# Attention and gated MLP on one core: a written-out engine order planned with other costs, another order of tanh and exp, and another start

## The chip, the cores and the metric

The kernel runs on one core of a Trainium2 chip. The time is device microseconds (us) of one execution, taken as the median of several. Before the change it is 603.34 us, the median of 3 runs (602.14 to 603.51).

## What is computed

Attention with capped scores over 4 batches, 12 heads, 448 positions and 64 features, and on its result a gated MLP with 768 features in, 1536 hidden and 768 out:

```python
scores = (q @ k.T) / sqrt(64)              # per batch and head, 448 x 448
scores = cap * tanh(scores / cap)
attn = exp(scores - scores.max(-1, keepdims=True))
attn = attn / (attn.sum(-1, keepdims=True) + 1e-09)
x = (attn @ v).transpose(0, 2, 1, 3).reshape(4 * 448, 768)
g = x @ w_gate
out = (g * (1 / (1 + exp(-g))) * (x @ w_val)) @ w_out
```

## The kernel before

**The work.** The 24 pairs of heads are taken two at a time in 12 "quads". A quad has 7 score tiles of 128 keys by 2 x 448 queries: three for each of the two pairs (numbers 1 to 6) and one shared by both for the last 64 keys (number 0, `MID`), which comes last. Of each tile TensorE makes the scores (`qk`, L886, float32) in one of two PSUM buffers `sc`; ScalarE takes the tanh of them (`tanh`, L890), which frees the buffer, and then the exponential (`exp`, L893). TensorE multiplies the exponentials with the values (`av`, L831, and `avt`, L912, for the shared tile), and sums them over the keys with ones (`sum`, L918) after VectorE has added three tiles together (`sa`, L813 and L815). VectorE empties the products' PSUM buffers (`xk`, L257); the sums go by DMA through a reshaping (`rl`, tile `r`), a reciprocal on VectorE (`rec`, L932) and two more DMAs (`rs`, `rld`) back to a multiplication on VectorE (`x`, L849).

On TensorE the order in the attention is a chain: after the first score tile of a quad come the `av` of the previous quad's first pair, then two score tiles, the `av` of its second pair, a score tile, the sums, two score tiles, `avt`, and the shared score tile.

The MLP follows, in float16 with high and low parts (L528 to L530: three products for each), by a fast matrix scheme of 7 products in place of 8, in 12 rounds for the first two matrices, then two passes for the third (L703 to L705). Its weights are read as 64-bit floats, narrowed to 32 bits on ScalarE and VectorE (`nA`, `nB`, `nC`, `n1`), stored to DRAM (`st`) and loaded again (`ld`, L466), then split in high and low halves (`wH` on ScalarE or VectorE, `wL` on VectorE). The narrowing of the first weights lies beside the attention.

**The order.** Class `Plan` lays all operations out by a list scheduling before anything is emitted. Each has a duration per engine that may do it, a priority (a time at which it is wanted), the operations that it waits for, and buffers that it takes. At each step the planner looks at the earliest start that any ready operation could have, and among those within 0.05 us of it takes the one with the earliest priority. The result is the order of instructions of every engine (SyncE issues nearly all the DMAs), and the engines keep it: an instruction that waits holds back all behind it on its engine. Durations and lags of the plan are constants of the code: `LAG` and `LAT` from the end of one operation to the start of another, `SWITCH` when TensorE goes to another kind of work, `ISSUE` for what one DMA operation costs on SyncE, `FAR` for what it takes longer to land. The grid of priorities in the attention is `QUAD` us to a quad.

**The start.** `warm` sends 9 products of a constant tile to TensorE (L294), gives the first 128 columns of the first keys to ScalarE's DMA queue (L280), and the load of the others follows the first queries on SyncE's (L789, L796).

**Buffers of the exponentials.** Each tile of a quad has a place among 11 (`w0` to `w5` and five `B` tiles), handed out at L764 to L773; the last quad uses `B` tiles only.

Of the kernel before, what the change touches and what calls it, by code (L numbers as in the profile page):

```python
# [8 lines left out]
F32 = mybir.dt.float32  # L9
# [7 lines left out]
P = 128  # L17
C = 112
S = 448
B = 4  # L20
# [19 lines left out]
WARM = 9  # L40


QUAD = 13.5
TAIL = 9.0
AHEAD = 14.0
NEAR = 4
# [8 lines left out]
NARROW_B = 40.0  # L55
NARROW_STEP_B = 7.4
HLOAD = {(0, 0): -14.0, (1, 0): -9.0, (0, 1): -4.0, (1, 1): 0.0}
SWITCH = 0.17


NARROWED = [4, "u", 5, "u", 6, "u", 7, 8, "u", 9, 10, "u", 11, "u"]
# [18 lines left out]
class Plan:  # L80


    LAT = 0.2
    LAG = {
        ("PE", "PE"): 0.0, ("ACT", "ACT"): 0.13, ("DVE", "DVE"): 0.13, ("POOL", "POOL"): 0.13, ("ACT", "DVE"): 0.16,
        ("DVE", "POOL"): 0.16, ("ACT", "POOL"): 0.18, ("POOL", "ACT"): 0.07, ("POOL", "DVE"): 0.08, ("ACT", "PE"): 0.25,
    }

    FAR = {"rl": 1.4, "rs": 1.4, "rld": 1.4}
    ISSUE = {"rld": 0.96}  # L90
    BIAS = {}
    SHIFT = dict.fromkeys(("c1", "c11", "cu", "c5", "c22", "c12", "oc1", "oc11", "ocu", "oc5", "oc22", "oc12", "wL", "wH"), -20.0) | {"gt": -20.0, "ga": -20.0, "va": -20.0, "sa": -15.0, "cp": -15.0, "rec": -15.0, "xk": -30.0}

# [10 lines left out]
    def run(self):  # L104
# [69 lines left out]
        while ready:  # L174
            t0, cands = 1e18, []
            for k in ready:
                o = ops[k]
                r = room(o) if o["alloc"] else 0.0
                if r is None:
                    continue  # L180
                best = None
                for t, d, e, x in o["opts"]:
                    s = max(t, r, free[e])
                    if e == "PE" and kind(k) != last:
                        s += SWITCH
                    c = s + x
                    if best is None or c < best[0]:
                        best = c, s, d, e
                cands.append((best[1], o["prio"], best[2], best[3], k))
                t0 = min(t0, best[1])  # L190
            if not cands:
                raise RuntimeError("the buffers do not suffice")
            s, _, d, e, k = min((c for c in cands if c[0] <= t0 + 0.05), key=lambda c: (c[1], c[0]))
            o = ops[k]
            if e == "SP":
                b = max(s + 1.125, dma_free)
                free[e] = s + self.ISSUE.get(k[0], 0.48)
                dma_free = b + d
                end[k] = dma_free + 0.73 + self.FAR.get(k[0], 0.0)
            else:  # L200
                free[e] = s + d
                end[k] = s + d
                if e == "PE":
                    last = kind(k)
            eng[k] = e
            for tag, readers in o["alloc"]:
                held[tag].append(readers)
            order.append((s, len(order), k, e))
            o["start"] = s
            o["eng"] = e  # L210
            del ready[k]
            for u in users.get(k, ()):
                nleft[u] -= 1
                if nleft[u] == 0:
                    enter(u)
# [6 lines left out]
def tile_capped_attention_gated_mlp(ctx: ExitStack, tc: tile.TileContext, qd, kd, vd, cap, eye, w1, w2, out):  # L222
# [21 lines left out]
    def st(shape, dtype, tag):  # L244
        return pool(tag).tile(shape, dtype, tag=tag, name=tag, bufs=BUFS[tag])
# [29 lines left out]
    icapr = nc.scalar.alloc_register("icapr")  # L275

    def warm():
        u = QUADS[0][0]
        T["rk", u] = st([P, S], F32, "c10")
        nc.scalar.dma_start(T["rk", u][:, :P], kd[u][:, :P])  # L280
        nc.scalar.dma_start(cap1[:, 0:1], cap)
        nc.gpsimd.dma_start(capb, cap.to_broadcast([P, 1]))
        z = nc.const_aps.tensor(1.0, (P, S), mybir.dt.bfloat16)
        nc.gpsimd.memset(ones, 0.0)
        for i in range(2):
            nc.gpsimd.memset(ones[:, 48 * i : 48 * i + 16], 2.0**-X_UP)
            nc.gpsimd.memset(ones[D * i : D * i + D, D + 16 * i : D + 16 * i + 16], 2.0**-X_UP)
        nc.gpsimd.memset(sq, 0.0)
        y = const.tile([P, 1], F32, name="tiny")
        nc.vector.memset(y, 0.0)  # L290
        nc.scalar.activation(y, y, AF.Tanh)
        o = pt([P, 512], "av")
        for i in range(WARM):
            nc.tensor.matmul(o[:, :S], lhsT=z[:, :P], rhs=z, start=True, stop=True)  # L294
# [29 lines left out]
        op(key, prio, {"ACT": us}, fn, deps + [spare])  # L324


    mm_us = 6 * 188 / 1000.0
    pair_us = 10.6 * mm_us / 7
    quad_at = [6.0 + QUAD * q for q in range(len(QUADS))]
    t = quad_at[-1] + QUAD + TAIL  # L330
# [92 lines left out]
    def blocks(w):  # L423
        g0, g1 = 2 * w * NCC, (2 * w + 1) * NCC
        for c in range(HALF):
# [14 lines left out]
            for p, (_, _, _, z) in PROD.items():  # L440

                def high(e, z=z, c=c):
                    T["xs", z, w, c] = x_half(("XH", z, w, c), home(z, w, c))
                    copy(e, T["xs", z, w, c][:, 0], T["raw", z, w, c])

                def low(e, z=z, c=c):
                    sub(e, T["xs", z, w, c][:, 1], T["raw", z, w, c], T["xs", z, w, c][:, 0])

                raw = ("x", {"B11": g0 + c, "B21": g0 + c + HALF, "B22": g1 + c + HALF}[z]) if z[0] == "B" else (z, w, c)
                order = prod_at[w, w, p] - AHEAD + 0.3 * c  # L450
                op(("XH", z, w, c), order, {"ACT": 0.57, "DVE": 0.39}, high, [raw], [(home(z, w, c), [("p", LAST[w], w, p)])])
                op(("XL", z, w, c), order + 0.01, {"DVE": 0.62}, low, [("XH", z, w, c)])
                if z in PLAIN:
                    n = 3 * PLAIN.index(z) + c
                    square(("qx", z, w, c), 2, win_at[3] + 10.0 * n + 5.0 * w, 0.58, lambda z=z, c=c: T["xs", z, w, c][:, 0], [("p", 3 + n // 2, 1, 4)], ("XH", z, w, c))

    def step(s):
        f, ws = STEPS[s]
# [44 lines left out]
            op(key("S", n), at[1 if n < 3 else 2] - [0, 12.5, 11.3, 13.8, 12.6][n], {"DVE": 0.52}, lambda e, n=n: comb(e, n), deps, alloc)  # L503
        for half in range(2):
            if 1 in ws:
                square(key("q", half), 0, at[0] - 6.0 + 2.0 * half, 0.85, lambda half=half: gate(half).rearrange("p a b -> p (a b)"), full[half], ("XH", "B11", s // NFC, 0))
        last = [2, 5, 3, 4]
        for n in range(4):
            tw = at[n] - 8.8
# [6 lines left out]
        for w in ws:  # L516
# [40 lines left out]
            for b in range(2):  # L557
# [19 lines left out]
                op(key("gt", w, b), z + 1.0, {"ACT": 0.56}, gt, [k("c12" if b else "c11")], [("th", [key("va", w, b)])])  # L577
                deps = [key("gt", w, b), k("c22")] + ([] if b else [("p", s, w, 4)])
                op(key("va", w, b), max(end + 0.2, z + 2.2), {"DVE": 0.62}, va, deps)
                square(("qh", g, f), 3, max(end, z + 2.0) + 1.0, 0.58, lambda b=b, w=w: T["cc", s, w, b], [key("va", w, b)], ("XH", "B11", 0, 0) if s < NFC - 1 else ("oH", 0, 1, 0))  # L580
                op(("hst", g, f), max(end, z + 2.0) + 1.2, {"SP": 0.64}, hst, [key("va", w, b)])

    NP = NDM // 2
# [23 lines left out]
    def outs(pr):  # L607
# [54 lines left out]
        for n, (p, d) in enumerate(OUT_ORDER):  # L662
# [11 lines left out]
            dep = [("st", "o", a, d, j) for j in range(2)]  # L674
            op(("ld", "o", pr, p, d), tp - 24.0, {"SP": 1.09}, load, dep, [(home_, [("wL", "o", pr, p, d)] + [("qo", p, d)] * pr)])
            if pr:
                square(("qo", p, d), 1, tp - 6.5, 0.85, lambda p=p, d=d: T["wf", "o", 1, p, d].rearrange("p a b -> p (a b)"), [("ld", "o", 1, p, d)], ("oH", 1, p, 0))

            def wH(e, p=p, d=d, n=n):
                T["wh", "o", pr, p, d], T["wl", "o", pr, p, d] = w_slots(wtag(4 * len(STEPS) + n))  # L680
# [75 lines left out]
    def spot(q, i):  # L756

        return (i - 1) % NT
# [2 lines left out]

        return quad_at[q] + (QUAD * (1.3 + 0.3 * n) if q < len(QUADS) - 1 else QUAD + 2.0 + 2.3 * n)

    TAGS, idle = {}, [f"w{n}" for n in range(6)] + ["B60", "B61", "B62", "B70", "B71"]  # L764
    for q in range(len(QUADS)):
        if q == len(QUADS) - 1:
            idle = [x for x in idle if x[0] == "B"] + ["B22", "B32", "B52"]
        old = TAGS.get(q - 1, [])
        TAGS[q] = [None] * NT
        for i in sorted(range(NT), key=lambda i: spot(q, i)):  # L770
            TAGS[q][i] = idle.pop(0)
            if old and i in (2, 4, MID):
                idle += [x for x in {2: old[1:4], 4: old[4:], MID: old[:1]}[i] if x[0] == "B" or q < len(QUADS) - 1]  # L773

    def pair(u, q):
        upper = u == QUADS[q][1]
# [12 lines left out]
            nc.sync.dma_start(T["rq", u], qd.rearrange("n p s -> (n p) s")[z : z + P])  # L789

        def loadk(e):
            if not joint and (q or upper):
                T["rk", u] = st([P, 6, P], F32, "wf").rearrange("p a b -> p (a b)")[:, :S] if upper else st([P, S], F32, f"c1{q % 2}")

            z = slice(0 if q or upper else P, S)
            nc.sync.dma_start(T["rk", u][:, z], kd[u][:, z])  # L796

        qks = sorted([("qk", q, i) for i in [MID] + own], key=lambda x: spot(q, x[2]))
        slot = lambda n: [(f"A4{q % 3}" if joint else "wf" if upper else f"c{n}{q % 2}", qks)]
# [59 lines left out]
    def quad(q):  # L859
# [12 lines left out]
        op(("loadv", q), quad_at[q] - 4.0, {"SP": 1.6}, loadv, alloc=[(f"B4{q % 2}", [("avt", q)])])  # L872

        for i in range(NT):
            tag = TAGS[q][i]

            def qk(e, i=i):
                z = T["sc", q, i] = pt([P, 2, 512], "sc")
# [23 lines left out]
            op(("qk", q, i), z, {"PE": 0.75}, qk, deps, [("sc", [("tanh", q, i)])])  # L902
            users = [("av", w[0], (i - 1) % 3)] if i != MID else [("avt", q)]
            users += [("sum", q)] if i == MID else [("sa", w[0], (i - 1) % 3 // 2)]
            op(("tanh", q, i), z + 1.0, {"ACT": 0.92}, tanh, [("qk", q, i)], [(tag, users)])
            op(("exp", q, i), z + 2.8, {"ACT": 0.95}, expo, [("tanh", q, i)])

        def avt(e):
            for h in range(2):
# [27 lines left out]

        tz = av_at(q, 2) + 2.0
        op(("avt", q), av_at(q, 2) - 0.5, {"PE": 0.75}, avt, [("exp", q, MID), ("loadv", q), ("av", u, 2), ("av", v, 2)])
        op(("sum", q), av_at(q, 2), {"PE": 1.15}, sums, [("sa", u, 1), ("sa", v, 1), ("exp", q, MID)], [("b2", [("cp", q)])])  # L940
        op(("cp", q), av_at(q, 2) + 1.0, {"DVE": 0.35}, part, [("sum", q)], [(f"c2{q % 2}", [("rl", q)])])
        op(("rl", q), tz + 0.1, {"SP": 0.2}, rl, [("cp", q)], [("r7", [("rs", q)])])
        op(("rec", q), tz + 3.0, {"DVE": 0.2}, rec, [("rl", q)])
# [154 lines left out]
    for q in range(len(QUADS) + 1):  # L1098
        now = [("qk", q, i) for i in sorted(range(NT), key=lambda i: spot(q, i))] if q < len(QUADS) else []
        if not q:  # L1100
            line += now
            continue
        u, v = QUADS[q - 1]
        avs = lambda z: [("av", z, j) for j in range(3)]
        line += now[:1] + avs(u) + now[1:3] + avs(v) + now[3:4] + [("sum", q - 1)] + now[4:6] + [("avt", q - 1)] + now[6:]
    for a, b in zip(line, line[1:]):
        plan.ops[b]["deps"].append(a)
    order = plan.run()
# [140 lines left out]
```

## Time and profile before

| | |
|---|---|
| median of 3 runs | 603.34 us |
| the profiled execution | 604.18 us |
| its span, first to last instruction | 602.3 us |
| TensorE matmul busy | 591.7 us, 98% |
| VectorE busy | 505.9 us, 84% |
| ScalarE busy | 418.4 us, 69% |
| chain that ended last | PE 84%, DMA 6%, DVE 5%, ACT 2% |

PE is TensorE (PEld its weight loads), DVE is VectorE, ACT is ScalarE, POOL is GpSimd, SP is SyncE; SPq is SP's own queue of DMA issues. "L886" is line 886 of the kernel. A matmul counts as busy until its modelled end, and consecutive matmuls overlap, so the busy time of PE says less than the starts of its rows.

### The profile page before, as it was taken

Reading aid. Unit: us, or ns where it says so; the run is one execution under the profiler, and the core shown is the slowest. Engines: PE = TensorE matmul, PEld = TensorE weight load, DVE = VectorE, ACT = ScalarE, POOL = GpSimd, SP = SyncE. Lnnn points to the kernel's source line nnn. Section 1 sums busy time; section 2 is a strip of 40 time slices with the busy share of each in tenths; the row PEclk is TensorE's granted clock in tenths of the full one; section 3 lists DMA queues with packets and bytes.
Section 4 is the critical chain, followed back from the end, with each engine's and each line's share of the span. In section 5 each row is a group of like instructions: output and inputs, shape, how many; then the busy total and the mean of one; then the engine's idle time right before and its main releaser. Section 6 shows DMA issues by size and latency. Waiting matters only on the chain.

```text
span 602.3 us, 9584 instructions
## 1 busy us (share of the span) xinstructions
PE 591.7 (98%) x3333; PEld 279.8 (46%) x3333; DVE 505.9 (84%) x869; ACT 418.4 (69%) x725; POOL 1.6 (0%) x11
## 2 busy tenths in 40 slices
PE   7999999999999999999999999999999999999997
PEld 2333333333345555555555555555455555555553
DVE  2678899899898998888989888989979999898840
ACT  6999989899858855756648476656757766685611
POOL 1000000000000000000000000000000000000000
PEclk9999999999999999999999999999999999999999
DMA  8676676755423365877786766586968598546121
GB/s 252 207 237 192 186 223 212 217 153 149 126 86 101 125 173 153 265 203 229 198 239 215 217 211 190 171 274 206 347 235 319 170 331 287 192 135 234 35 78 66
DMA packets 69598, 118.08 MB, mean 196 GB/s; under 512 B 13604, under 2 KB 47524, under 8 KB 69541
## 3 DMA queue, kind: packets, MB, share of 16 engines
q1 hardware_dynamic: 69362, 117.32, 61.4%
q8 instruction: 28, 0.46, 0.3%
q14 instruction: 30, 0.24, 0.1%
q10 hardware_dynamic: 146, 0.07, 0.0%
q0 software_dynamic: 32, 0.00, 0.0%
HBM read 81.79 MB, written 35.48 MB: 195 GB/s over the span
## 4 chain that ended last, share of the span: by engine, by line
PE 84%; DMA 6%; DVE 5%; ACT 2%; SPq 2%; issue 1%; ACTq 0%; DVEq 0%
PE b L528 10%; PE b L530 10%; PE b L529 10%; PE sc L886 7%; PE b L704 7%; PE b L703 7%; PE b L705 7%; PE av L831 6%; PE om L528 4%; PE om L530 4%; PE om L529 4%; DMA w<-w 3%; DMA r<-c 2%; PE b L918 2%; PE av L912 1%; PE om L704 1%
## 5 line engine op out<-in xcount | busy, mean ns | idle before, releaser
L528 PE MATMUL b<-A,w 128*128 128x448 f16 x252 | 88.8, 352 | 0.4 <-ACT c L255 0.4
L529 PE MATMUL b<-A,w 128*128 128x448 f16 x252 | 88.8, 352 | 0.0
L530 PE MATMUL b<-A,w 128*128 128x448 f16 x252 | 88.8, 352 | 0.0
L528 PEld LDWEIGHTS <-w 128*128 128x128 f16 x504 | 49.3, 98 | 46.8 <-issue 0.7
L529 PEld LDWEIGHTS <-w 128*128 128x128 f16 x504 | 49.3, 98 | 46.4 <-issue 0.7
L530 PEld LDWEIGHTS <-w 128*128 128x128 f16 x504 | 49.3, 98 | 46.0
L255 ACT ACTIVATE c<-b 128x448 f32<-128x448 f32 x54 | 29.0, 538 | 44.4 <-PE b L705 22.9
L528 PE MATMUL om<-B,w 128*128 128x448 f16 x144 | 50.8, 352 | 0.0
L529 PE MATMUL om<-B,w 128*128 128x448 f16 x144 | 50.8, 352 | 0.0
L530 PE MATMUL om<-B,w 128*128 128x448 f16 x144 | 50.8, 352 | 0.0
L886 PE MATMUL sc<-c,c 64*128 64x448 f32 (+1 forms) x192 | 45.2, 577 | 2.4 <-ACT w L890 1.5
L546 DVE TENSOR_TENSOR c<-c,b 128x448 f32<-128x448 f32 x60 | 37.1, 619 | 8.6 <-PE b L530 3.2
L262 DVE TENSOR_TENSOR A<-A,A 128x448 f16<-128x448 f32 (+3 forms) x55 | 43.7, 823 | 0.1
L255 ACT ACTIVATE w<-B 128x768 f16<-128x768 f32 x32 | 26.9, 840 | 22.9 <-PE b L705 17.9
L890 ACT ACTIVATE w<-sc 128x896 f32<-128x896 f32 x42 | 36.9, 917 | 7.2 <-PE sc L886 7.0
L890 ACT ACTIVATE B<-sc 128x896 f32<-128x896 f32 x42 | 36.9, 921 | 5.0 <-PE sc L886 4.9
L262 DVE TENSOR_TENSOR w<-B,w 128x768 f16<-128x768 f32 x39 | 37.0, 953 | 2.2 <-ACT w L255 2.2
L893 ACT ACTIVATE B<-B 128x896 f32<-128x896 f32 x42 | 38.4, 959 | 0.1
L893 ACT ACTIVATE w<-w 128x896 f32<-128x896 f32 x42 | 38.2, 955 | 0.1
L704 PE MATMUL b<-A,w 128*128 128x448 f16 x108 | 38.1, 352 | 0.0
L528 PE MATMUL b<-B,w 128*128 128x448 f16 x108 | 38.1, 352 | 0.0
L530 PE MATMUL b<-B,w 128*128 128x448 f16 x108 | 38.1, 352 | 0.0
(138 smaller groups left out, 1233.3 us busy)
## 6 DMA issues: line engine op xcount, KB each, us to landing
w<-w SPq DMA_DIRECT2D x72, 384.0 KB, 3.7
hidden<-c SPq DMA_DIRECT2D x48, 224.0 KB, 3.1
B<-w_S SPq DMA_DIRECT2D x24, 384.0 KB, 4.3
w<-wf SPq DMA_DIRECT2D x16, 384.0 KB, 4.9
B<-w SPq DMA_DIRECT2D x15, 384.0 KB, 3.4
th<-parts SPq DMA_DIRECT2D x48, 112.0 KB, 2.9
A<-hidden SPq DMA_DIRECT2D x12, 448.0 KB, 5.7
B<-hidden SPq DMA_DIRECT2D x12, 448.0 KB, 3.8
```

What stands on the lines that cost most here:

```text
L255: nc.scalar.activation(out_, in_, AF.Copy, scale=1.0 if scale is None else scale)
L262: ENG[e].tensor_tensor(out_, a, b, op=ALU.subtract)
L528: nc.tensor.matmul(o, lhsT=wh, rhs=xh, start=first, stop=False, skip_group_check=True)
L529: nc.tensor.matmul(o, lhsT=wl, rhs=xh, start=False, stop=False, skip_group_check=True)
L530: nc.tensor.matmul(o, lhsT=wh, rhs=xl, start=False, stop=end, skip_group_check=True)
L546: nc.vector.tensor_tensor(z, z, T["ps", s, w, b][:, :S], op=ALU.add)
L703: nc.tensor.matmul(o, lhsT=wh, rhs=xh, start=first, stop=False, skip_group_check=True)
L704: nc.tensor.matmul(o, lhsT=wl, rhs=xh, start=False, stop=False, skip_group_check=True)
L705: nc.tensor.matmul(o, lhsT=wh, rhs=xl, start=False, stop=end, skip_group_check=True)
L886: nc.tensor.matmul(z[rows, h, :S], lhsT=T["rk", w][r, keys], rhs=T["rq", w][r], start=True, stop=True)
L890: nc.scalar.activation(T["t", q, i], T["sc", q, i][:, :, :S], AF.Tanh, scale=icapr)
L893: nc.scalar.activation(T["t", q, i], T["t", q, i], AF.Exp, scale=capr)
```

## The change

The planner's constants are replaced, the priority of `exp` moves from 2.8 to 5.0 us behind its tile's grid time, the places of the exponentials become a plain ring of 11, and the last quad uses seven `B` tiles. The keys of the first pair are loaded whole by SyncE behind the queries. The 9 warm passes read a tile of zeros that VectorE fills.

```diff
-QUAD = 13.5
+QUAD = 13.1
-SWITCH = 0.17
+SWITCH = {"sc": 0.206, "av": 0.15, "sh": 0.16, "sum": 0.0, "mm": 0.16}
     LAT = 0.2
-    LAG = {
-        ("PE", "PE"): 0.0, ("ACT", "ACT"): 0.13, ("DVE", "DVE"): 0.13, ("POOL", "POOL"): 0.13, ("ACT", "DVE"): 0.16,
-        ("DVE", "POOL"): 0.16, ("ACT", "POOL"): 0.18, ("POOL", "ACT"): 0.07, ("POOL", "DVE"): 0.08, ("ACT", "PE"): 0.25,
-    }
-    FAR = {"rl": 1.4, "rs": 1.4, "rld": 1.4}
-    ISSUE = {"rld": 0.96}
+    LAG = {("PE", "PE"): 0.0, ("ACT", "PE"): 0.08, ("DVE", "PE"): 0.08}
+    LAG |= {(a, b): 0.04 for a in ("ACT", "DVE") for b in ("ACT", "DVE")}
+    OVERLAP = {"ACT": 0.1, "DVE": 0.085}
+    FAR = {"rl": 2.0, "rs": 2.0, "rld": 2.0, "ld": 1.5}
+    ISSUE = {"rld": 1.26, "loadv": 2.45, "rl": 0.65, "rs": 0.4, "ld": 0.45, "st": 0.54}
...
-                        s += SWITCH
+                        s += SWITCH[last]
...
-                free[e] = s + self.ISSUE.get(k[0], 0.48)
+                free[e] = s + self.ISSUE.get(k[0], 0.48) * (2 if k[0] == "loadq" and d > 1.0 else 1)
...
-                free[e] = s + d
+                free[e] = s + d - self.OVERLAP.get(e, 0.0)
...
     def warm():
-        u = QUADS[0][0]
-        T["rk", u] = st([P, S], F32, "c10")
-        nc.scalar.dma_start(T["rk", u][:, :P], kd[u][:, :P])
...
-        z = nc.const_aps.tensor(1.0, (P, S), mybir.dt.bfloat16)
+        z = st([P, 2 * S], F32, "B20").bitcast(mybir.dt.bfloat16)[:, :S]
+        nc.vector.memset(z, 0.0)
...
-    mm_us = 6 * 188 / 1000.0
+    mm_us = 6 * 189 / 1000.0
...
-    TAGS, idle = {}, [f"w{n}" for n in range(6)] + ["B60", "B61", "B62", "B70", "B71"]
-    ...
+    RING = [*(f"w{n}" for n in range(6)), "B60", "B61", "B62", "B70", "B71"]
...
-            z = slice(0 if q or upper else P, S)
-            nc.sync.dma_start(T["rk", u][:, z], kd[u][:, z])
+            nc.sync.dma_start(T["rk", u], kd[u])
...
-            tag = TAGS[q][i]
+            tag = (["B22", "B32", "B52", "B60", "B61", "B62", "B70"][spot(q, i)] if q == len(QUADS) - 1 else RING[(NT * q + spot(q, i)) % len(RING)])
...
-            op(("tanh", q, i), z + 1.0, {"ACT": 0.92}, tanh, [("qk", q, i)], [(tag, users)])
-            op(("exp", q, i), z + 2.8, {"ACT": 0.95}, expo, [("tanh", q, i)])
+            op(("tanh", q, i), z + 1.0, {"ACT": 0.917}, tanh, [("qk", q, i)], [(tag, users)])
+            op(("exp", q, i), z + 5.0, {"ACT": 0.953}, expo, [("tanh", q, i)])
...
-        op(("sum", q), av_at(q, 2), {"PE": 1.15}, sums, ...
+        op(("sum", q), av_at(q, 2), {"PE": 1.27}, sums, ...
```

The planned durations of the squares that watch the range of the numbers grow by 0.08 us as well. TensorE's chain in the attention is the same.

## Rows read from the trace of the kernel before

**Rows 1.** Waits of PE in two stretches, 15 to 168 us and 168 us on.

```profile
PE sc L886 <- ACT B L890: 0.8, 1, 0.8
PE av L831 <- DVE B L257: 0.6, 1, 0.6
PE av L831 <- DVE A L257: 0.5, 1, 0.5
...
PE b L528 <- ACT c L255: 0.4, 1, 0.4
```

**Rows 2.** Windows: stretch, its length, busy (count) by engine, PEclk, DMA share, GB/s.

```profile
158.00:171.00 13.00, 11.65 (x89) 4.41 (x89) 13.00 (x22) 10.89 (x18) 0.00 (x0) 1.00 0.32 97
...
300.00:400.00 100.00, 100.00 (x530) 51.72 (x529) 88.71 (x175) 62.99 (x154) 0.00 (x0) 1.00 0.69 216
```

**Rows 3.** Timeline of PE: start, us, engine, line, operation, count.

```profile
0.78 3.52 PE L294 MATMUL av<-const-bfloat16-1.0 128*128 128x448 bf16 x9 [0.78 <-PEq L1238]
4.22 3.91 PE L886 MATMUL sc<-c,c 64*128 64x448 f32 x12
...
14.96 1.02 PE L886 MATMUL sc<-c,c 64*128 64x448 f32 x4
...
28.02 1.02 PE L886 MATMUL sc<-c,c 64*128 64x448 f32 x4
...
80.26 1.02 PE L886 MATMUL sc<-c,c 64*128 64x448 f32 x4
...
93.92 1.02 PE L886 MATMUL sc<-c,c 64*128 64x448 f32 x4
...
106.98 1.02 PE L886 MATMUL sc<-c,c 64*128 64x448 f32 x4
...
120.41 1.02 PE L886 MATMUL sc<-c,c 64*128 64x448 f32 x4
...
168.09 0.36 PE L528 MATMUL b<-A,w 128*128 128x448 f16 x1
```

**Rows 4.** Timeline of ACT over the first quad.

```profile
6.14 0.92 ACT L890 ACTIVATE w<-sc 128x896 f32<-128x896 f32 x1 [2.90 <-PE sc L886]
7.21 0.92 ACT L890 ACTIVATE w<-sc 128x896 f32<-128x896 f32 x1 [0.16 <-PE sc L886]
8.02 1.78 ACT L893 ACTIVATE w<-w 128x896 f32<-128x896 f32 x2
9.70 0.91 ACT L890 ACTIVATE w<-sc 128x896 f32<-128x896 f32 x1
...
13.07 1.73 ACT L890 ACTIVATE w<-sc 128x896 f32<-128x896 f32 x2
```

**Rows 5.** Groups by line: busy us, mean ns | idle before; the nearest to a fill.

```profile
L257 DVE CAST A<-A 128x448 f16<-128x448 f32 x15 | 5.4, 385 | 0.0
...
L288 POOL MEMSET sq<- 128x192 f32 x1 | 0.3, 258 | 0.1
...
L290 DVE MEMSET tiny<- 128x1 f32 x1 | 0.1, 59 | 0.8 <-PEq L1238 0.8
```

**Rows 6.** DMA issues: one SP row, and two of KB and median us to landing.

```profile
1.19 0.41 SPq L796 DMA_DIRECT2D c<-kd  x1
...
c<-kd SPq DMA_DIRECT2D x11, 224.0 KB, 4.2
...
c<-kd SPq DMA_DIRECT2D x1, 160.0 KB, 2.9
```

**Rows 7.** Waits of all engines, 145 to 170 us.

```profile
DVE w L257 <- DMA wf<-w: 2.0, 1, 2.0
ACT w L255 <- DMA wf<-w: 1.6, 1, 1.6
```

**Rows 8.** Chain of work that ended last, in order of time: start, us, what.

```profile
67.41 6.07 DMA r<-c
...
148.60 3.72 DMA wf<-w
```

More of the change, by code (lines that the diff above doesn't have):

```diff
@@ L454, in blocks @@
                     n = 3 * PLAIN.index(z) + c
-                    square(("qx", z, w, c), 2, win_at[3] + 10.0 * n + 5.0 * w, 0.58, lambda z=z, c=c: T["xs", z, w, c][:, 0], [("p", 3 + n // 2, 1, 4)], ("XH", z, w, c))
+                    square(("qx", z, w, c), 2, win_at[3] + 10.0 * n + 5.0 * w, 0.66, lambda z=z, c=c: T["xs", z, w, c][:, 0], [("p", 3 + n // 2, 1, 4)], ("XH", z, w, c))
     def step(s):
@@ L505, in step @@
             if 1 in ws:
-                square(key("q", half), 0, at[0] - 6.0 + 2.0 * half, 0.85, lambda half=half: gate(half).rearrange("p a b -> p (a b)"), full[half], ("XH", "B11", s // NFC, 0))
+                square(key("q", half), 0, at[0] - 6.0 + 2.0 * half, 0.93, lambda half=half: gate(half).rearrange("p a b -> p (a b)"), full[half], ("XH", "B11", s // NFC, 0))
         last = [2, 5, 3, 4]
@@ L579, in step @@
                 op(key("va", w, b), max(end + 0.2, z + 2.2), {"DVE": 0.62}, va, deps)
-                square(("qh", g, f), 3, max(end, z + 2.0) + 1.0, 0.58, lambda b=b, w=w: T["cc", s, w, b], [key("va", w, b)], ("XH", "B11", 0, 0) if s < NFC - 1 else ("oH", 0, 1, 0))
+                square(("qh", g, f), 3, max(end, z + 2.0) + 1.0, 0.66, lambda b=b, w=w: T["cc", s, w, b], [key("va", w, b)], ("XH", "B11", 0, 0) if s < NFC - 1 else ("oH", 0, 1, 0))
                 op(("hst", g, f), max(end, z + 2.0) + 1.2, {"SP": 0.64}, hst, [key("va", w, b)])
@@ L676, in outs @@
             if pr:
-                square(("qo", p, d), 1, tp - 6.5, 0.85, lambda p=p, d=d: T["wf", "o", 1, p, d].rearrange("p a b -> p (a b)"), [("ld", "o", 1, p, d)], ("oH", 1, p, 0))
+                square(("qo", p, d), 1, tp - 6.5, 0.93, lambda p=p, d=d: T["wf", "o", 1, p, d].rearrange("p a b -> p (a b)"), [("ld", "o", 1, p, d)], ("oH", 1, p, 0))
             def wH(e, p=p, d=d, n=n):
@@ L762, in av_at @@
         return quad_at[q] + (QUAD * (1.3 + 0.3 * n) if q < len(QUADS) - 1 else QUAD + 2.0 + 2.3 * n)
-    TAGS, idle = {}, [f"w{n}" for n in range(6)] + ["B60", "B61", "B62", "B70", "B71"]
[L765 to L773, printed above, removed]
+    RING = [*(f"w{n}" for n in range(6)), "B60", "B61", "B62", "B70", "B71"]
     def pair(u, q):
@@ L791, in loadk @@
         def loadk(e):
-            if not joint and (q or upper):
+            if not joint:
                 T["rk", u] = st([P, 6, P], F32, "wf").rearrange("p a b -> p (a b)")[:, :S] if upper else st([P, S], F32, f"c1{q % 2}")
-            z = slice(0 if q or upper else P, S)
-            nc.sync.dma_start(T["rk", u][:, z], kd[u][:, z])
+            nc.sync.dma_start(T["rk", u], kd[u])
         qks = sorted([("qk", q, i) for i in [MID] + own], key=lambda x: spot(q, x[2]))
@@ L939, in quad @@
         op(("avt", q), av_at(q, 2) - 0.5, {"PE": 0.75}, avt, [("exp", q, MID), ("loadv", q), ("av", u, 2), ("av", v, 2)])
-        op(("sum", q), av_at(q, 2), {"PE": 1.15}, sums, [("sa", u, 1), ("sa", v, 1), ("exp", q, MID)], [("b2", [("cp", q)])])
+        op(("sum", q), av_at(q, 2), {"PE": 1.27}, sums, [("sa", u, 1), ("sa", v, 1), ("exp", q, MID)], [("b2", [("cp", q)])])
         op(("cp", q), av_at(q, 2) + 1.0, {"DVE": 0.35}, part, [("sum", q)], [(f"c2{q % 2}", [("rl", q)])])
@@ L1104, in tile_capped_attention_gated_mlp @@
         avs = lambda z: [("av", z, j) for j in range(3)]
-        line += now[:1] + avs(u) + now[1:3] + avs(v) + now[3:4] + [("sum", q - 1)] + now[4:6] + [("avt", q - 1)] + now[6:]
+        line += now[0:1] + avs(u) + now[1:3] + avs(v) + now[3:4] + [("sum", q - 1)] + now[4:6] + [("avt", q - 1)] + now[6:7]
     for a, b in zip(line, line[1:]):
```

## The prediction, as it was put on record

> **What bounds the kernel now.** I read the waits of TensorE first, since the page gives it 98% of the span. From 168 us on, that is through the whole MLP, it waited once, for 0.4 us [rows 1]; its products follow each other at 100 / 530 = 0.189 us [rows 2]. No order of the other engines makes this stretch shorter by more than that 0.4. So what can be won lies ahead of 168.09 us, where the first product of the MLP starts [rows 3].
>
> There I read TensorE's timeline. The first score tile of a quad starts at 14.96, the next quad's at 28.02: 13.06 us to a quad, back to back, since no wait of it in 15 to 168 us lies there [rows 1, 3]. The changed kernel has the same chain of the same products, so 13.06 stays. What stands beside it: one quad of 93.92 - 80.26 = 13.66 and one of 120.41 - 106.98 = 13.43, so 0.60 and 0.37 lost, and in the last quad waits of 0.8 for ScalarE and 0.6 for VectorE [rows 1, 3]. These sum to 2.37 us. The rest of the loss is ahead of 14.96, where TensorE runs dry between tiles because ScalarE's tanh frees the two score buffers too slowly [rows 4].
>
> **The start: a later warm-up.** The first pass started at 0.78; the 9 passes took 3.52 us and the first score tile followed at 4.22 [rows 3]. At 0.39 us a pass for as many columns as a 0.189 us product of the MLP, the clock was at the lower of its two levels there, 1.2 GHz. Now the passes need VectorE's fill. VectorE was free to start at 0.8 (its small fill waited 0.8, [rows 5]). A fill of 448 two-byte elements is in no row. From below it is the fill of one element, 0.06; from above GpSimd's fill of 192 elements, 0.258 x 448 / 192 = 0.60; I take the row with the same shape on the same engine, the cast of 128x448 to float16, 0.385 [rows 5]. The first pass then starts at about 1.2, 0.42 later (0.1 to 0.63), and everything behind it on TensorE too. The Trainium skill (VectorE: DVE Perf Modes, section "Zero memsets can be issued as uint32 (trn2)") has a rule against this edit: a fill costs one cycle per element whatever its type, not fewer for two-byte ones. By it the fill is some 0.47 us as an estimate, and the saving 0.08 smaller than by the row; no row before shows such a fill.
>
> The keys go from two queues to one. ScalarE's queue loses an issue, for which nobody waits: its first tanh waited 2.90 us for TensorE [rows 4]. SyncE issues as many DMAs as before, one of them 64 KB larger. The part that it loaded, 160 KB issued at 1.19, landed 2.9 later, at 4.09 [rows 6]. The whole keys move bytes that moved beside it before, so I take 4.1 to 4.3, hidden under warm passes that now end past 4.6. The upper bound is the 4.2 us of later key loads [rows 6]: 5.4, which would add some 0.75.
>
> **The start: tanh in front.** A grid step was 13.5 / 7 = 1.93, so exp of a tile (grid + 2.8) went ahead of the next tanh (grid + 1.93 + 1); in the trace it runs tanh, tanh, exp, exp. With step 1.87 and exp at grid + 5.0, up to two later tanh go ahead of an exp (1.87 x 2 + 1 = 4.74), if their scores are there. Worked through with two score buffers, ScalarE's order becomes: tanh 0, 1, exp 0, tanh 2, 3, exp 1, tanh 4, exp 2, tanh 5, exp 3, tanh 6. From rows 4 a tanh takes 0.92 and the next operation starts 0.80 to 0.81 after its start (two in 1.73); an exp passes on after (9.70 - 8.02) / 2 = 0.84. From the start of tanh 0 to the end of tanh 5: 1.07 (tanh 1, held by TensorE as at 7.21) + 0.80 + 0.84 + 0.80 + 0.80 + 0.84 + 0.80 + 0.09 (the small exp for eps) + 0.84 + 0.92 = 7.80. That releases the first tile of the second quad 0.05 later. Before, this took 14.96 - 6.14 = 8.82, so 0.97 is won. With tanh 0 at 6.14 + 0.42 = 6.56, the tile starts at 14.41 in place of 14.96: **-0.55** (-0.88 to -0.34, by the bounds of the fill; +0.4 if the order stayed as it is).
>
> From there the chain goes on at 13.06 if the exponentials keep up. A quad gives ScalarE 7 x (0.80 + 0.84) = 11.5 us of work, 1.6 less than TensorE's. The exps 3 to 5 that are put off lie under the 2.4 and more that TensorE spends on the first pair's products.
>
> **The stalls.** All four come from transfers that the plan takes for shorter than they are. In the last quad ScalarE stood 1.6 us and VectorE 2.0 before splits of weights whose load had not landed [rows 7]. Behind ScalarE's was a tanh, hence the 0.8; behind VectorE's the emptying of a product buffer, hence the 0.6. That load took 3.72 us [rows 8]; the old plan gives it 1.125 + 1.09 + 0.73 = 2.95, the new one 1.5 more, 4.45. So the splits are placed after the landing, and I count 1.4 as won. The other two come behind the reshaped sums: 6.07 us from issue to landing [rows 8]; the old plan has 1.125 + 0.2 + 0.73 + 1.4 = 3.46, the new one 4.06, plus what it now reckons for the four issues of the values ahead on SyncE (2.45 in place of 0.48). That is still short of 6, so I count half of the 0.97: 0.49. Together **-1.9** (0 to -2.37).
>
> What is late next is ScalarE and VectorE at the hand-over: VectorE was busy 13.00 of 13 us from 158 to 171 [rows 2], and the MLP is to begin 2.4 us earlier. I cost this at nothing, since part of that work moves into VectorE's 2.0 us of waiting; its price is a rival.
>
> **The other edits.** The ring of 11 frees each place behind products that the chain puts ahead of its next writer, so no tanh waits; 0, with a bound of one wait as ScalarE's, 0.8. The MLP's order is planned anew with other lags. TensorE waited 0.4 in 430 us under the old costs; I take 0 for the difference, between -0.4 and +1.6 (one wait as long as ScalarE's). The end is the same products and stores.
>
> **The sum.** -0.55 - 1.9 = -2.45. The profiled execution took 604.18 (span 602.3 and 1.9 around it), 0.84 above the median; it would become 601.7. Against the median, 603.34 - 2.45 = **600.9**. Its own range is 599.7 (-0.88 - 2.37 - 0.4) to 602.1 (a stall of 1.2 left over).
>
> **Rivals.**
> - *The hand-over takes it back.* The attention ends earlier, but the last norms, splits and sums are VectorE's, full there, and TensorE waits for them in the first rounds. For: 13.00 of 13. Against: no wait of TensorE after 168 but one. It can take all of the 1.9 and leave the start: 602.8, or 603.3 with that. 22%.
> - *The stalls stay.* The plan doesn't do what it says where it matters: a load of 6 us stays beyond 4.06, and a moved order meets another late transfer. Half of the 2.37 remains in other places and the start is won only with the upper fill: 603.34 - 0.34 - 1.19 = 601.8. 18%.
> - *Slower: split and cast work put in front of tanh.* The new plan believes ScalarE to pass on 0.1 us earlier after each operation, 1.4 a quad, and so gives it more casts and splits in the attention. Each that waits there holds a tanh, and with two score buffers TensorE soon after. The price is that of the quad at 106.98, 0.37; in 11 quads 4.1, and 603.34 - 0.55 + 4.1 - 1.4 = 605.5. It decides from 5 to 6 such quads on ((0.55 + 1.4) / 0.37). Against: ScalarE has 1.6 us of air in a quad. 12%.
>
> **How the numbers follow.** A difference under 0.3%, 1.8 us, can't be told from none here: faster is below 601.5, slower above 605.2. The forecast has 48%, mostly below 601.5; the first rival lies in the middle, the second around 602, partly below 601.5. That gives faster 0.50, same 0.40, slower 0.10. The range that holds 8 in 10 goes from 599.4 (all stalls and the 0.4 gone, and the runs' own spread) to 603.4, to take in the first two rivals; above that lies most of the third.
>
> **What would show it.** Warm passes from 1.2, the first score tile near 4.6, the second quad's first tile near 14.4 with ScalarE's rows as tanh, tanh, exp, tanh, tanh, exp; eleven periods of 13.06 with no waits for `wf`; the MLP's first product near 165.6 and its last 2.4 earlier than before. The prediction is wrong if the second quad starts past 15, if waits of ScalarE on VectorE or DMA appear ahead of tanh, or if TensorE's waits after the hand-over add up to more than 1 us.

## The result: slower by 1.4%

The changed kernel takes 611.66 us (median of 4 runs, 609.19 to 612.47) against 602.96 (4 runs, 602.14 to 603.51; the 603.34 that the forecast starts from is the median of three of them): a ratio of 1.0139 [1.0106, 1.0172]. 600.9 was forecast, in a range that ended at 603.4. The profiled execution of the changed kernel took 612.47, with a span of 610.7, that is 8.4 more than the span of before.

The page of the changed kernel gives the busy time of each engine, its share of the span and the number of instructions:

```profile
span 610.7 us, 9542 instructions
...
PE 592.4 (97%) x3333; PEld 279.1 (46%) x3333; DVE 516.2 (85%) x904; ACT 399.3 (65%) x691; POOL 1.6 (0%) x11
```

TensorE does the same 3333 products. VectorE has 10.3 us more work than before (505.9) and ScalarE 19.1 less (418.4).

The timeline of TensorE answers to [rows 3]. The columns are start, duration, engine, line, operation and tiles; the bracket is idle time ahead and who ended it:

```profile
1.16 3.54 PE L291 MATMUL av<-B 128*128 128x448 bf16 x9 [1.16 <-DVE tiny L287]
4.63 1.77 PE L873 MATMUL sc<-c,c 64*128 64x448 f32 x8
...
13.31 1.02 PE L873 MATMUL sc<-c,c 64*128 64x448 f32 x4 [0.76 <-ACT w L877]
...
165.86 0.36 PE L525 MATMUL b<-A,w 128*128 128x448 f16 x1
```

The MLP starts 2.23 us earlier than before (168.09), close to the 2.45 forecast. ScalarE's timeline of the first quad, beside [rows 4], has the order that was worked out, tanh, tanh, exp, tanh, tanh, exp, tanh (L877 is tanh, L880 exp):

```profile
5.70 1.73 ACT L877 ACTIVATE w<-sc 128x896 f32<-128x896 f32 x2 [2.91 <-PE sc L873]
7.31 0.95 ACT L880 ACTIVATE w<-w 128x896 f32<-128x896 f32 x1
8.15 1.72 ACT L877 ACTIVATE w<-sc 128x896 f32<-128x896 f32 x2
9.74 0.97 ACT L880 ACTIVATE w<-w 128x896 f32<-128x896 f32 x1
10.58 0.94 ACT L877 ACTIVATE w<-sc 128x896 f32<-128x896 f32 x1
```

VectorE's timeline has the fill that the warm passes wait for, and it is shorter than the 0.385 taken:

```profile
0.86 0.24 DVE L280 MEMSET B<- 128x224 uint32 x1 [0.86 <-PEq L1225]
```

The loss is in the MLP. The waits of TensorE from 165 us on (total, times, longest), where [rows 1] had one of 0.4:

```profile
PE om L525 <- DVE c L543: 5.0, 7, 1.4
PE b L525 <- DVE c L256: 1.9, 2, 1.6
PE b L525 <- ACT c L254: 0.8, 1, 0.8
PE om L525 <- ACT c L254: 0.4, 1, 0.4
```

Counted from the starts of the products (distance above the usual 0.189 us), the gaps of the MLP add up to 10.5 us in 14 places, against 0.57 in one place before. The account of the span closes: -2.23 at the MLP's start, +9.93 in its gaps, +0.7 after its last product (4.8 us to the end before, 5.5 now): +8.4. In the windows view of 165 to 450 us, where all gaps lie (duration, then busy time and count of PE, PEld, DVE, ACT, POOL, granted clock, DMA share, GB/s), first the kernel before:

```profile
165.00:450.00 285.00, 284.59 (x1526) 146.57 (x1523) 255.46 (x481) 183.16 (x412) 0.00 (x0) 1.00 0.65 201
```

and the changed one:

```profile
165.00:450.00 285.00, 276.78 (x1457) 141.58 (x1456) 256.64 (x503) 162.80 (x369) 0.00 (x0) 1.00 0.64 192
```

The granted clock is 1.00 in both, so the gaps are no matter of the clock. VectorE is busy for 90% of the stretch, 1.2 us more than before, and ScalarE has 20 us less to do, so the amount of work explains no 10 us of gaps. What VectorE waits for in this stretch on DMA tells more:

```profile
DVE wf L1018 <- DMA w<-wf: 12.8, 13, 2.4
```

The same line in the kernel before:

```profile
DVE wf L1031 <- DMA w<-wf: 1.1, 4, 0.5
```

L1018 (L1031 before) is `add` in `narrow_out`: it sums two narrowed quarters of the third matrix and writes over one of them, so it has to wait until the store (`st`) of that quarter to DRAM has landed. The timeline around the gap of 1.58 us at 421 shows how that reaches TensorE (SPq is SyncE's queue):

```profile
416.20 0.43 SPq L1013 DMA_DIRECT2D w<-wf  x1
...
419.35 0.55 DVE L968 SCALAR_TENSOR_TENSOR wf<-wf,w 128x384 int32<-128x384 int32 x1
...
421.23 0.35 PE L527 MATMUL b<-A,w 128*128 128x448 f16 x1
...
421.86 0.56 DVE L1018 TENSOR_TENSOR wf<-wf 128x384 f32<-128x384 f32 x1 [1.96 <-DMA w<-wf]
422.33 0.61 DVE L543 TENSOR_TENSOR c<-c,om 128x448 f32<-128x448 f32 x1
423.00 0.35 PE L525 MATMUL om<-B,w 128*128 128x448 f16 x1 [1.42 <-DVE c L543]
```

VectorE was done at 419.90 and stood 1.96 us before `add`. The emptying of TensorE's product buffer (an eviction, L543) is queued behind `add` on VectorE, and TensorE's next product waits for that buffer. The chain that ended last has stores of the same kind, and one of the hidden values (start, duration):

```profile
276.82 5.48 DMA hidden<-c
...
338.44 3.86 DMA w<-wf
...
387.33 3.76 DMA w<-wf
...
416.20 5.56 DMA w<-wf
```

The planner gives a store of a quarter at least 1.125 + 0.55 + 0.73 = 2.4 us and no `FAR`. It lets one transfer follow another, and most of these stores come 0.45 us behind a load of 1.09, so that the plan lands them after 1.125 + 1.09 + 0.55 + 0.73 - 0.45 = 3.05. Those in the chain took 3.8 to 5.6, and the view of DMA issues (count, size, median from issue to landing) has for the group of 24, of which the trace tells 8 landings:

```profile
w<-wf SPq DMA_DIRECT2D x24, 192.0 KB, 3.9
```

Six of the 14 gaps, 5.9 of the 10.5 us, come behind such a store in the chain: those at 272, 298, 347, 396, 421 and 428. The largest gap, 1.73 at 281, comes behind the store of hidden values, for which the plan has 1.125 + 0.64 + 0.73 = 2.5:

```profile
282.42 0.62 DVE L256 COPY c<-b 128x448 f32<-128x448 f32 x1 [1.28 <-ACT A L319]
...
283.10 0.35 PE L525 MATMUL b<-A,w 128*128 128x448 f16 x1 [1.56 <-DVE c L256]
```

L256 writes over the stored buffer. The store landed at 282.30, and an operation of ScalarE, which this row names, ended at 282.31, so the trace does not tell which of the two was waited for last. Of the rest, 1.15 us lie between 167 and 201, where the attention hands over, and 1.7 at 372, 439 and 448 where the chain's last transfer ahead of the gap is a load.

### The profile page after: what moved, and what is told of

Its sections match the earlier page's. It is cut to its first block, busy times and chain, and to the rows that moved or that the text cites. A ratio compares the mean times of both kernels' runs of the same rounds, so it can differ in the third digit from the quotient of the medians.

```text
span 610.7 us, 9542 instructions
## 1 busy us (share of the span) xinstructions
PE 592.4 (97%) x3333; PEld 279.1 (46%) x3333; DVE 516.2 (85%) x904; ACT 399.3 (65%) x691; POOL 1.6 (0%) x11
## 4 chain that ended last, share of the span: by engine, by line
PE 57%; DVE 22%; DMA 11%; issue 5%; ACT 3%; SPq 1%; DVEq 0%; ACTq 0%
PE sc L873 8%; PE av L818 7%; PE b L702 7%; PE b L701 7%; PE b L700 7%; DMA w<-wf 5%; PE b L525 4%; PE b L527 3%; PE b L526 3%; DVE w L964 3%; DVE c L543 3%; DVE wf L968 2%; DMA hidden<-c 2%; DVE w L261 2%; PE b L905 2%
## 5 line engine op out<-in xcount | busy, mean ns | idle before, releaser
L254 ACT ACTIVATE c<-b 128x448 f32<-128x448 f32 x49 | 26.3, 536 | 49.6 <-PE b L702 29.4
L319 ACT ACTIVATE A<-c 128x448 f16<-128x448 f32 x48 | 27.5, 572 | 21.8 <-DVE c L563 21.2
L877 ACT ACTIVATE B<-sc 128x896 f32<-128x896 f32 x42 | 37.6, 923 | 5.1 <-PE sc L873 4.9
L877 ACT ACTIVATE w<-sc 128x896 f32<-128x896 f32 x42 | 37.3, 916 | 4.8 <-PE sc L873 4.6
L543 DVE TENSOR_TENSOR c<-c,b 128x448 f32<-128x448 f32 x60 | 36.9, 616 | 2.8 <-ACT A L319 1.4
L880 ACT ACTIVATE w<-w 128x896 f32<-128x896 f32 x42 | 38.9, 955 | 0.1
L880 ACT ACTIVATE B<-B 128x896 f32<-128x896 f32 x42 | 38.6, 957 | 0.2
L558 ACT ACTIVATE th<-c 128x448 f32<-128x448 f32 x48 | 26.1, 565 | 18.7 <-DVE c L543 18.4
```

The costliest lines, as they stand in the source:

```text
L543: nc.vector.tensor_tensor(z, z, T["ps", s, w, b][:, :S], op=ALU.add)
L877: nc.scalar.activation(T["t", q, i], T["sc", q, i][:, :, :S], AF.Tanh, scale=icapr)
L880: nc.scalar.activation(T["t", q, i], T["t", q, i], AF.Exp, scale=capr)
```

## Experiments

Two causes stood against each other. One is the stores (theory B of the expectations): the plan believes them landed too early (3.05 for most, against a median of 3.9). The other is the pace (theory A): the new plan takes `OVERLAP` off VectorE and ScalarE and shortens `LAG`, so that little is left between the planned and the real end of an operation. Theory C blames the longer landing of loads. A further question is whether the new start or the order of tanh and exp plays a part, and what is left of the forecast's gain once the MLP is mended.

Ratios are to the kernel before with their 95% interval. The first time is a median, or a single run where it says so; the other columns are of the profiled execution. The MLP's start is its first product, and "VectorE for stores" is its wait ahead of `add` between 165 and 450 us. Those of e3 and e4 are of executions of 614.25 and 612.32 us, where their runs spread over 614.25 to 621.49 and 609.20 to 619.35. Only e6 (that of before) and e9 (that of e5) keep another kernel's order; the others have theirs planned anew, so none changes a landing or a lag in an order that stays the same.

| kernel | us | ratio | MLP's start | gaps in the MLP | VectorE for stores |
|---|---|---|---|---|---|
| before | 602.96 | | 168.09 | 0.6 | 1.1 |
| changed | 611.66 | 1.0139 [1.0106, 1.0172] | 165.86 | 10.5 | 12.8 |
| e1, before with `OVERLAP` | 614.71 | 1.0198 [1.0171, 1.0226] | 172.20 | 6.4 | 0.4 |
| e2, changed, stores 1.5 longer | 603.91 | 1.0015 [0.9999, 1.0031] | 165.83 | 3.1 | no row |
| e3, changed without `OVERLAP` | 618.60 | 1.0278 [1.0241, 1.0315] | 164.25 | 14.9 | 3.9 |
| e4, changed without `FAR` of loads | 614.94 | 1.0176 [1.0088, 1.0263] | 172.06 | 5.5 | 0.4 |
| e5, e2 and hidden longer too | 602.49 | 0.9992 [0.9976, 1.0008] | 166.59 | 1.2 | no row |
| e6, before with the new start | 603.09 | 1.0004 [0.9990, 1.0017] | 167.06 | 0.6 | 1.2 |
| e7, changed, exp early as before | 610.41, one run | | 165.43 | 9.9 | 11.0 |
| e8, e1 and all `FAR` | 606.07 | 1.0055 [1.0034, 1.0077] | 167.27 | 2.4 | 0.2 |
| e9, e5 with the constant warm tile | 603.03 | 0.9997 [0.9981, 1.0013] | 165.03 | 1.2 | no row |
| e10, changed with the old `LAG` | 604.88, one run | | 166.68 | 3.1 | 11.2 |
| e11, changed, stores 0.75 longer | 604.60, one run | | 166.00 | 1.7 | 7.3 |

**e1: the pace alone, on the kernel before.**

```diff
-                free[e] = s + d
+                free[e] = s + d - {'ACT': 0.1, 'DVE': 0.085}.get(e, 0.0)
```

> The kernel before with one line more: ScalarE and VectorE count as free 0.1 and 0.085 us ahead of an operation's end in the plan. Theory A (the faster engines in the plan fill VectorE and ScalarE so full, with some 30 more evictions on VectorE, that any late transfer in the MLP is never made up): the MLP's waits of TensorE appear, 6 to 10 us of them, and the time is 607 to 611. Theory B (the sums of the third matrix wait for stores that the plan takes for landed): the same, if the slack that hid them goes with this line. Theory C (the longer landing of loads, FAR for ld, is at fault): no more than 1 us of waits, 601 to 603.

This one line costs 12 us, more than was expected under A and B. The attention pays too: the MLP starts 4.1 us later than before. In the MLP VectorE hardly waits for stores here; it and ScalarE wait for loads of weights, which have no `FAR` in the old plan. Waits of both for DMA from 165 to 450 us:

```profile
ACT w L971 <- DMA w<-w: 11.1, 6, 3.4
ACT wf L255 <- DMA w<-w: 10.1, 7, 2.0
DVE wf L259 <- DMA w<-w: 8.2, 9, 1.5
...
DVE wf L1031 <- DMA w<-wf: 0.4, 2, 0.2
```

But the kernel before waited longer for the same loads, and had one gap:

```profile
ACT wf L255 <- DMA w<-w: 22.8, 22, 2.7
...
ACT w L971 <- DMA w<-w: 13.4, 13, 2.1
DVE wf L259 <- DMA w<-w: 7.0, 10, 1.3
```

So these waits are no longer than before; what is new is that gaps follow behind them. The largest of e1's gaps, 1.94 us at 279, comes behind this row of VectorE:

```profile
278.16 0.36 DVE L259 TENSOR_SCALAR wf<-w 128x384 f32<-128x384 f32 x1 [1.37 <-DMA w<-w]
```

Another 1.6 of the 6.4 us lie at 200 to 208, where VectorE's rows follow each other without a wait; there it is full, as theory A has it.

**e2: the stores alone.** In the changed kernel only the planned landing of stores is put 1.5 us later.

```diff
-    FAR = {"rl": 2.0, "rs": 2.0, "rld": 2.0, "ld": 1.5}
+    FAR = {"rl": 2.0, "rs": 2.0, "rld": 2.0, "ld": 1.5, "st": 1.5}
```

> The changed kernel, with 1.5 us more for the landing of a store (FAR for st) in the plan. Theory B: VectorE's waits for stores ahead of the sums, 12.8 us in the changed kernel, fall under 4, TensorE's waits in the MLP from 8.9 to under 3, and the time to 601 to 604. Theory A: little changes, 608 to 612.

7.8 us of the 8.7 lost are back, as forecast under theory B. VectorE waits for no store ahead of `add` any more, and TensorE's waits from 165 us on are

```profile
PE om L525 <- DVE c L543: 0.9, 2, 0.7
PE om L525 <- DVE c L256: 0.7, 1, 0.7
PE b L525 <- DVE c L256: 0.3, 1, 0.3
```

Of the 3.06 us of gaps left, 1.15 lie between 167 and 201 us, where the attention hands over, and 1.9 at 425 to 441, where splits wait for loads of the hidden values (`hld`).

**e3: the new plan without `OVERLAP`.**

```diff
-    OVERLAP = {"ACT": 0.1, "DVE": 0.085}
+    OVERLAP = {}
```

> The changed kernel, without the overlap of ScalarE and VectorE in the plan (free only at an operation's end). Theory A: the MLP's waits of TensorE go, under 1.5 us are left, and with the earlier start the time is 599 to 602. Theories B and C: waits of 6 us and more stay, 606 to 611.

The number given under theory A was missed, and the one under B and C too. The MLP starts earlier than in any other run, but its gaps are the largest. They are not waits for stores (3.9 us) in the first place; TensorE's waits from 165 us on are for splits:

```profile
PE b L525 <- ACT w L254: 3.6, 1, 3.6
PE b L527 <- DVE B L261: 2.1, 1, 2.1
PE b L702 <- DVE B L261: 2.1, 1, 2.1
```

Here the plan itself, with engines slower than the real ones, leaves TensorE idle: by the starts and ends that class `Plan` gives the operations, for some 17 us in the MLP, in the changed kernel for 0.4. After the first of these gaps (3.78 us at 179) the products followed each other at 0.37 us until 189, with the granted clock at 0.50, the lower of its two levels (1.2 GHz); so that gap cost more than its length. The window has

```profile
184.00:189.00 5.00, 4.61 (x13) 1.95 (x14) 3.67 (x6) 3.02 (x8) 0.00 (x0) 0.50 0.30 95
```

Taking `OVERLAP` away does not bring the old plan back, for the other constants go with it.

**e4: the new plan without the later loads.**

```diff
-    FAR = {"rl": 2.0, "rs": 2.0, "rld": 2.0, "ld": 1.5}
+    FAR = {"rl": 2.0, "rs": 2.0, "rld": 2.0}
```

> The changed kernel, without the 1.5 us more that loads of weights take to land (FAR for ld). Theory C: the MLP's waits go, 600 to 602. Theories A and B: they stay, 608 to 612; ahead of the MLP the waits for weights of the first round may come back, some 1.4 us.

Theory C's number was missed; the time is as long as e1's, with the same late start of the MLP, 172.06 (e1: 172.20). Between 165 and 450 us ScalarE's wait for loads is the largest row of DMA, though shorter than the 22.8 of the kernel before:

```profile
ACT wf L254 <- DMA w<-w: 14.8, 8, 4.1
```

The margin for loads is worth 6.2 us at the MLP's start. VectorE now waits 0.4 us for stores, with no margin for them either, which theory B had not expected: that error of the plan is a wait of 12.8 us or of next to nothing, by the order around it.

**e5 and e9: all stores and hidden loads later, and the old warm tile on top.** e5 adds to e2, and e9 takes e5 and goes back to the constant tile for the warm passes:

```diff
+    FAR = {"rl": 2.0, "rs": 2.0, "rld": 2.0, "ld": 1.5, "st": 1.5, "hld": 1.5, "hst": 0.5}
...
-        z = st([P, 2 * S], F32, "B20").bitcast(mybir.dt.bfloat16)[:, :S]
-        nc.vector.memset(z, 0.0)
+        z = nc.const_aps.tensor(1.0, (P, S), mybir.dt.bfloat16)
```

> The changed kernel with longer landings in the plan for stores (st, 1.5 us more), for the loads of the hidden rows (hld, 1.5) and for their stores (hst, 0.5). Theory B (transfers that the plan takes for landed hold VectorE, and no slack is left that makes it good): of TensorE's 3.1 us of MLP gaps with the longer store alone, the 1.8 between 425 and 441 us go, where splits of hidden rows waited for their loads; the time is 601 to 602.5. Theory A (VectorE too full): gaps of 3 us stay in other places, 603.5 to 605.

> As e5_store_hidden_far, but the warm passes read the constant again, which is there before VectorE can fill a tile. The first pass starts at 0.78 and the first score tile at 4.2 or where the keys land, some 0.4 earlier; if nothing else takes it back the time is 0.2 to 0.4 below that of e5_store_hidden_far, 600.7 to 602.2.

e5 is the best version and equals the kernel before within its interval. Its 1.16 us of gaps all lie between 168 and 201. In e9 the first pass starts at 0.78 in place of 1.16, and the second quad's first tile at 13.84 in place of e5's

```profile
14.39 1.02 PE L873 MATMUL sc<-c,c 64*128 64x448 f32 x4 [0.76 <-ACT w L877]
```

The last product of e9 is 1.55 us earlier than that of e5 (595.04 against 596.59), but 6.1 us pass from there to its end against 4.3 in e5. In the medians (603.03 and 602.49) no gain from the earlier warm-up can be told; the 0.2 to 0.4 us expected of e9 were missed.

**e6 and e7: the start alone, and the order of exp alone.** e6 is the kernel before with the keys whole on SyncE and the filled warm tile; e7 is the changed kernel with exp at its old priority.

```diff
-        z = nc.const_aps.tensor(1.0, (P, S), mybir.dt.bfloat16)
+        z = st([P, 2 * S], F32, "B20").bitcast(mybir.dt.bfloat16)[:, :S]
+        nc.vector.memset(z, 0.0)
...
-            if not joint and (q or upper):
+            if not joint:
...
-            z = slice(0 if q or upper else P, S)
-            nc.sync.dma_start(T["rk", u][:, z], kd[u][:, z])
+            nc.sync.dma_start(T["rk", u], kd[u])
```

In e7, the priority of exp goes from `z + 5.0` back to `z + 2.8`.

> The kernel before with the new start alone: the first keys whole on SyncE, and the warm passes on a tile that VectorE fills. Its order is otherwise that of before. The first pass starts near 1.16 in place of 0.78 and the first score tile near 4.6 in place of 4.22; with exps still in pairs the second quad starts 0.2 to 0.5 later than at 14.96, and the time is 602.8 to 603.4. If the start were behind the MLP's waits, which no theory here says, these would appear: 605 and more.

> The changed kernel with the old priority of exp (2.8 us behind its tile). If tanh in front is what brings the second quad forward, ScalarE runs tanh, tanh, exp, exp in the first quad and the second quad's first tile goes from 13.3 to 14.1 to 14.6. Theory B leaves the MLP's gaps at 6 us or more, since the stores are as in the changed kernel: 608 to 613.

The start alone makes no difference that can be measured. Its passes start at 1.16 and its second quad at 14.94, where before had 14.96. e7 has ScalarE's old order, tanh, tanh, exp, exp, and its second quad starts later than e5's:

```profile
14.81 1.02 PE L873 MATMUL sc<-c,c 64*128 64x448 f32 x4
```

It keeps the gaps of the MLP (9.9), so the order of exp is not what makes them. (Of these 9.9 us, 1.7 are products at 0.37 us from 398 to 402 behind a gap of 2.15, where the granted clock is 0.57.)

**e8: the kernel before with `OVERLAP` and every `FAR`.**

```diff
-    FAR = {"rl": 1.4, "rs": 1.4, "rld": 1.4}
+    FAR = {"rl": 2.0, "rs": 2.0, "rld": 2.0, "ld": 1.5, "st": 1.5, "hld": 1.5, "hst": 0.5}
```

(beside the line of e1)

> The kernel before with the overlap of ScalarE and VectorE in the plan, as in e1_before_overlap, and with longer landings for all transfers that they wait for (rl, rs, rld 2.0; ld, st, hld 1.5; hst 0.5). Theory B (an order of engines planned at their true pace needs the true landing of transfers): of e1's losses, 4 us ahead of the MLP and 6.4 in it, the MLP starts before 169 and has gaps of under 3.5 us, of which some 2 between 190 and 205 are the plan's own; 602.5 to 606. Theory A (overlap alone fills the engines too full): 610 to 615 as e1.

Later landings take back 8.6 of e1's 12 us (614.71 to 606.07) in a plan that has nothing else of the change. Of the 2.4 us of gaps left, 2.1 lie ahead of 204, where VectorE's rows follow each other without a wait; the largest, 1.3, is one that e1 has too. Real pace and true landings belong together in this planner.

**e10: the changed kernel with the old `LAG`.** The lags go back from 0.04 and 0.08 to 0.13 to 0.25.

```diff
-    LAG = {("PE", "PE"): 0.0, ("ACT", "PE"): 0.08, ("DVE", "PE"): 0.08}
-    LAG |= {(a, b): 0.04 for a in ("ACT", "DVE") for b in ("ACT", "DVE")}
+    LAG = {
+        ("PE", "PE"): 0.0, ("ACT", "ACT"): 0.13, ("DVE", "DVE"): 0.13, ("POOL", "POOL"): 0.13, ("ACT", "DVE"): 0.16,
+        ("DVE", "POOL"): 0.16, ("ACT", "POOL"): 0.18, ("POOL", "ACT"): 0.07, ("POOL", "DVE"): 0.08, ("ACT", "PE"): 0.25,
+    }
```

> The changed kernel with the old lags between engines (0.13 to 0.25 us in place of 0.04 to 0.08). If the shorter lags were what takes the slack away, the MLP's gaps fall under 4 us and the time to 605; by theory B they stay at 6 and more, with VectorE's waits for stores ahead of the sums over 8 us, 608 to 613.

The number given under theory B was missed, and this changed the explanation. VectorE still waits for the stores, nearly as long as in the changed kernel (12.8):

```profile
DVE wf L1020 <- DMA w<-wf: 11.2, 14, 2.0
```

and yet TensorE waits little from 165 us on:

```profile
PE b L527 <- ACT c L256: 1.5, 1, 1.5
PE om L527 <- DVE c L545: 0.3, 1, 0.3
PE om L527 <- ACT c L256: 0.2, 1, 0.2
```

So late stores need not make a gap. Over half of e10's 3.1 us is one gap of 1.7 at 421, and there VectorE's rows follow each other without a wait from 416 to 422. The reading that fits is that late stores make gaps where the evictions behind them are planned to end just in time, and that the long lags keep these earlier. It rests on one run, which has another order too; which operations the lags moved was not followed further.

**e11: half the margin for stores**, `"st": 0.75`.

> The changed kernel with half of the longer store landing (0.75 us in place of 1.5). Theory B: VectorE's waits for stores lie between the changed kernel's 12.8 us and e2_store_far's none, 2 to 8, and the MLP's gaps between 10.5 and 3.1; 604 to 609.

The plan now lands most of these stores after 3.8 us, close to the 3.9 measured. VectorE's waits go from 12.8 to 7.3 us, as expected, but the gaps from 10.5 to 1.7, below the range given and below e2's 3.1:

```profile
DVE wf L1018 <- DMA w<-wf: 7.3, 10, 1.7
```

Again the gaps are no share of the waits: some slack swallows a wait whole.

## Why the prediction was wrong

- **The step that failed** is "The MLP's order is planned anew with other lags. ... I take 0 for the difference, between -0.4 and +1.6". It measured +9.9, and the prediction's own sign of being wrong, more than 1 us of waits after the hand-over, came out. The upper bound was one wait as long as ScalarE's in the attention; there were 14 gaps. The argument was that TensorE waited 0.4 in 430 us under the old costs, and that says how good the old order was, not what the plan knew: e1 shows that the old landings with engines at real pace cost 12 us. The prediction compared a planned landing with its row for loads and for the reshaped sums, but not for the stores. The trace of before has their row, against 3.0 planned for most:

```profile
w<-wf SPq DMA_DIRECT2D x24, 192.0 KB, 3.8
```

- **The mechanism**: the changed plan lands the stores of quarters after 3.05 us for most where they take 3.9, VectorE stands ahead of the sums that overwrite them, and evictions come late behind it: 5.9 of the 10.5 us of gaps. By the chain, a store of hidden values lies behind another 1.7. The loss goes with later planned stores (e2, e11) and with the old lags (e10, though VectorE's waits stay). Before, the same landings were in the plan and VectorE waited 1.1 us. By the plan's own times a sum stood on average 1.9 us behind the planned landing of the quarter that it overwrites; in the changed kernel and in e10 it is 0.9. e1, which changes only the pace, has gaps of 6.4 us, behind loads and where VectorE is full. That the lags work by the slack they leave to the evictions is the reading that fits these runs; no run shows it by itself. How much of what e2, e10 and e11 give back is due to the landing or the lag, and how much to the other order that comes with it, stays open: e4 does nothing for the stores, and VectorE's wait for them falls to 0.4 all the same.
- **Start of the MLP.** -2.45 was forecast and -2.23 measured, but the two terms are off against each other. *The start* was forecast at -0.55 and came at 13.31 - 14.96 = -1.65. The order of ScalarE was right; the passes began at 1.16 and the first score tile at 4.63, as forecast (1.2 and 4.6). The rest is when TensorE's pace rises: in this execution the first 8 score products took 1.77 us, in e2, with the same order, 2.73, and in e5 the first 12 took 3.91, as before the change. e5's second quad starts at 14.39, and 14.41 was forecast: the worked-out order holds, and the 1.1 us more in the changed kernel's trace is the luck of that execution. *The stalls* were forecast at -1.9. From the second quad to the MLP it is 152.55 us, 153.13 before: -0.58. The quad at 78.61 took 13.90, 0.84 over its 13.06, and in the last quad TensorE waited 1.1 us for VectorE. Part of the 2.37 was that one execution's own: e6, with the old order, needs 152.12. So a sum over one execution's stalls counted waits that the next one does not have.
- **The fill** took 0.24 us, not 0.385; it was issued as 224 four-byte words. The Trainium skill (VectorE: DVE Perf Modes, section "Zero memsets can be issued as uint32 (trn2)") says just this, that a fill of zeros can be issued at four bytes to an element; the estimate of 0.47 that the prediction drew from it was for the two-byte form. The row agrees with the page.
- **Rivals.** None named the mechanism, and none reached 611.66. The slower one looked for splits ahead of tanh in the attention; TensorE's waits for ScalarE there after the first quad are one of 0.2 us. The hand-over rival was no idle thought: once the MLP is mended (e5), 1.16 us of gaps lie between 168 and 201, against none in e6, and the MLP starts 0.47 earlier than in e6. The last products are at 596.59 and 596.52. What the changed plan wins ahead of the MLP it gives back there, which would be why even e5 is no faster. These numbers are of one execution each, and ahead of the MLP e6 and the kernel before, with the same order, differ by 1 us; so this is no closer than that.

## What to carry to other kernels

A planner's errors can cancel, as they seem to here: where it takes engines for slower than they are, its order has slack in it that hides transfer times planned too short. Whoever corrects the pace has to hold every planned landing against the trace in the same step, stores too where a buffer is overwritten in place behind them. Judge an order written by such a planner by which waits it would meet if each transfer came at its measured time, not by the few waits of the order that it replaces.

## What was not expected of the hardware

- The landing of a transfer doesn't follow its size here. In the changed kernel's DMA issues, the stores of the hidden values have 224 KB and land in 2.2 us (though one took 5.48), the narrowed quarters have 192 KB and take 3.9, as long as weights of twice the size. Before the change it was 3.1 and 3.8. Both stores go to DRAM over SyncE's queue; what parts them was not tried.

```profile
w<-w SPq DMA_DIRECT2D x72, 384.0 KB, 3.9
hidden<-c SPq DMA_DIRECT2D x48, 224.0 KB, 2.2
```

- The moment at which TensorE's pace rises at the start differs between executions of the same instructions by enough to move the second quad by 1.08 us (13.31 and 14.39), while the granted clock is given as 1.00 in both from 0 to 15 us. The pace of the products shows it, the granted clock does not. So the lower level that the prediction read from the 0.39 us of a warm pass rests on the pace alone.
